# Attention and two MLP layers on one Trainium2 core: expert groups of four for the whole first layer, weight conversions spread out, and the last block's outputs finished one after the other

## The chip, the core and the metric

The kernel runs on one core of one Trainium2 chip (trn2). A core has five engines, each with a queue of its own that runs strictly in order: TensorE (PE, matrix products; PEld is its weight loading), VectorE (DVE), ScalarE (ACT), GpSimd (POOL) and SyncE (SP, which here issues all DMA transfers). They wait for one another through semaphores. Matrix products go to PSUM, from which ACT and DVE read them.

The metric is the device time of one execution in microseconds (us). Several runs are made; their median counts.

## What is computed

Three stages follow each other on 2304 tokens (4 batches of 576) of width 512:

```python
scores = q @ k.T / 8                         # 4 batches x 8 heads, 576 x 64
keep   = scores >= rowmax(scores) - tau
x      = softmax(where(keep, scores, -1e9)) @ v
x      = g(x @ w1_in) @ w1_out               # g(h) = h * sigmoid(1.702 h), 512 -> 2048 -> 512
out    = max(0.01 h, h) @ w2_out             # h = x @ w2_in
```

The arithmetic is float32. The weights arrive as 64-bit floats.

## The kernel before

**Products in parts.** The products are taken in the format fp32r, and every operand is split into a high part (a cast to it) and a low part (the difference); so every product is made three times: high by high, low by high, high by low. In the names, `xh`/`xl` are the two parts of a layer's input, `wih`/`wil` of its input weights, `gh`/`gl` of the hidden values, `woh`/`wol` of its output weights. The cast is ACT's (L318, L294, L827), the difference mostly POOL's (L320, L297, L828).

**Attention** handles 16 head pairs. Its instructions stand in an order written out by hand: the table `START` gives a number to each step of each pair, and the steps are emitted by ascending number (`G20` is the load of an input-weight tile, `H0` and `H1` are hidden sums of the first layer, which already run among the last pair's steps). Three weight tiles are converted in attention (`CONVERTED`), three more are only loaded there (`STAGED`).

**The MLP layers** work on blocks of 512 tokens (`TB`; five blocks, the last of 256) and on hidden slices of 128 (`f`, 16 per layer). The slices are taken in groups (`GROUPS`): for each group, all five blocks go by, and for each block all slices of the group. One (group, block, slice) is a step. In step s, PE makes the hidden sums of step s (`hidden_sums`, L332: 12 matmuls) and then the output products of step s - 2 (`product`, L856 or, in layer 2, L858: 12 matmuls), since `LA` is 2. Between the two, ACT applies the nonlinearity (L820 or L823), DVE completes it (L821 or L824), ACT casts it to `gh`, POOL makes `gl`. After a block's last slice in a group, `collect` adds the output sums to an accumulator that lies where the block's input lay (L874 copies for the first group, L876 adds, L879 and `store` for the last group of layer 2). Layer 1 has groups of 2, 4, 4, 4 and 2 slices, layer 2 four groups of 4. An undisturbed step of 512 tokens is 24 matmuls of 512 columns.

**Weight conversion.** Each (slice, in or out) weight tile of 128 by 512 is loaded as 64-bit words (G, L261, into one of three staging buffers `w64`), and turned into float32 by integer operations in five parts: A on ACT (L275), B, C, D, K on DVE (L277, L279, L283, L287), all in a tile `wF` (two buffers); then H, the high part, on ACT (L294) and M, the low part, on POOL (L297). Two plans say in which steps the parts are emitted:

```python
    slow = dict(G=-4, A=0, B=1, C=1, D=2, K=2, H=3, M=3)
    fast = dict(G=-2, A=0, B=0, C=0, D=0, K=0, H=0, M=0)
```

The slow plan takes a new tile every second step; the fast one does a whole tile in every step, and is used where a stretch has too few steps for the slow one: for the first group's missing tile (step 0), for group 1's eight tiles (steps 1 to 8, beside group 0's ten steps), and for layer 2's first eight tiles (beside layer 1's last group, ten steps). `weight_parts` emits them: A to K and H stand in a step after the nonlinearity and ahead of the cast `gh` of that step. So the ACT queue holds in a fast step: nonlinearity, A, H (which waits for DVE's K), `gh`, splits.

**Splits of the input.** `splits(s)` emits the split of the next block's input in the first group of each layer, four chunks over the present block's steps; block 1 of layer 1 is split ahead of step 0.

**The end.** Block 4 has 256 tokens and, in layer 2, two output tiles of 128 tokens. Both lie in one PSUM tile. The last two products run one after the other, each over both outputs, and then both are added and stored (two transfers each).

What is written after the hand-ordered part may be placed by the program's scheduler among earlier instructions where nothing holds it; within an engine's queue the order is then fixed.

## Time and profile before

| quantity | us |
|---|---|
| runs: lowest, median, highest (3) | 1187.96, 1189.27, 1189.45 |
| the profiled execution's own time | 1188.86 |
| its span, first to last instruction | 1187.1 |
| PE busy in the span | 1133.6 (95%) |
| DVE busy | 663.6 (56%) |
| ACT busy | 586.3 (49%) |
| POOL busy | 586.3 (49%) |
| mean granted TensorE clock | 0.986 of full speed |

The profiled execution lies 0.41 us under the median, and its span 1.76 us under its own time; those 1.76 us lie around the span. A busy PE is not a PE at full speed: matmuls overlap in the records, and at a lower granted clock (1.2 instead of 2.4 GHz) a busy PE does half the work. In the profile, "chain" is the chain of waits that ended last, followed back from the last instruction; a timeline row gives in brackets the idle time ahead of an instruction and who ended it.

### The profile page before, as it was taken

What the parts mean: (1) busy time and instruction counts of PE and PEld (TensorE: products, weight loads), DVE (VectorE), ACT (ScalarE), POOL (GpSimd) and SP (SyncE); (2) the same over time, 40 slices, a digit from 0 to 9 for tenths busy, and PEclk for the clock granted to TensorE, in tenths of its full rate; (3) what the DMA queues carried; (4) which work ended last, traced back from release to release, by engine and by line L of the source; (5) the groups of instructions that cost most, each with busy time, mean ns of one, the idle gap of its engine ahead of it and who ended that gap; (6) DMA issues with size and microseconds to landing.
All of it is one profiled execution on the core that took longest, in us unless ns stands there. A gap on an engine that the chain in (4) does not pass through costs nothing.

```text
span 1187.1 us, 17037 instructions
## 1 busy us (share of the span) xinstructions
PE 1133.6 (95%) x6201; PEld 968.2 (82%) x6201; DVE 663.6 (56%) x1357; ACT 586.3 (49%) x1138; POOL 586.3 (49%) x519
## 2 busy tenths in 40 slices
PE   8998999999896799999999999889999999999997
PEld 7887898889884588888888888778888888888886
DVE  6999999999876633443452524843343352534232
ACT  6998989999884432332332322334433332332221
POOL 6787887877774423343343332455543333343221
PEclk8999999999997989999999999999999999999999
DMA  5332323221302201110110100211110110110022
GB/s 145 82 84 64 82 61 98 70 72 35 103 1 72 70 19 36 54 54 18 54 54 18 54 18 19 90 35 37 53 54 18 54 54 18 54 36 1 36 63 62
DMA packets 47619, 62.38 MB, mean 53 GB/s; under 512 B 10544, under 2 KB 39216, under 8 KB 47536
## 3 DMA queue, kind: packets, MB, share of 16 engines
q1 hardware_dynamic: 47536, 61.29, 18.3%
q8 instruction: 49, 0.80, 0.3%
q14 instruction: 34, 0.28, 0.1%
HBM read 47.71 MB, written 4.72 MB: 44 GB/s over the span
## 4 chain that ended last, share of the span: by engine, by line
PE 69%; DVE 14%; ACT 10%; issue 3%; POOL 2%; DMA 1%; SPq 0%; DVEq 0%; ACTq 0%; POOLq 0%
PE h L332 30%; PE y L858 17%; PE y L856 13%; ACT e L469 3%; PE pv L585 3%; DVE m L462 3%; DVE pp L490 2%; PE s L435 2%; PE pp L511 2%; ACT raw L533 1%; DVE wF L277 1%; DVE wF L279 1%; DVE wF L287 1%; DVE x L876 1%; ACT ptg1h L542 1%
## 5 line engine op out<-in xcount | busy, mean ns | idle before, releaser
L828 POOL TENSOR_TENSOR gl<-gf,gh 128x512 fp32r<-128x512 f32 (+1 forms) x160 | 205.6, 1285 | 511.2 <-ACT gh L827 476.7
L824 DVE TENSOR_TENSOR gf<-h,gf 128x512 f32<-128x512 f32 (+1 forms) x80 | 51.0, 638 | 239.8 <-ACT gf L823 239.8
L332 PE MATMUL h<-xh,wih 128*128 128x512 f32 (+1 forms) x640 | 160.6, 371 | 17.5 <-ACT xh L318 17.5
L821 DVE TENSOR_TENSOR gf<-h,gf 128x512 f32<-128x512 f32 (+1 forms) x80 | 50.9, 637 | 207.6 <-ACT gf L820 207.6
L332 PE MATMUL h<-xl,wih 128*128 128x512 f32 (+1 forms) x640 | 160.8, 372 | 2.5 <-POOL xl L320 2.3
L823 ACT ACTIVATE gf<-h 128x512 f32<-128x512 f32 (+1 forms) x80 | 44.5, 556 | 233.8 <-PE h L332 230.7
L332 PE MATMUL h<-xh,wil 128*128 128x512 f32 (+1 forms) x640 | 159.2, 371 | 0.0
L332 PEld LDWEIGHTS h<-xh,wih 128*128 128x128 f32 x640 | 114.8, 188 | 41.7 <-ACT xh L318 20.5
L820 ACT ACTIVATE gf<-h 128x512 f32<-128x512 f32 (+1 forms) x80 | 44.4, 555 | 201.8 <-PE h L332 201.7
L332 PEld LDWEIGHTS h<-xl,wih 128*128 128x128 f32 x640 | 114.9, 191 | 25.0 <-POOL xl L320 5.0
L332 PEld LDWEIGHTS h<-xh,wil 128*128 128x128 f32 x640 | 114.7, 190 | 20.4
L856 PE MATMUL y<-gh,woh 128*128 128x512 f32 (+1 forms) x320 | 119.6, 378 | 8.1 <-DVE x L876 5.5
L827 ACT CAST gh<-gf 128x512 fp32r<-128x512 f32 (+1 forms) x160 | 92.5, 578 | 59.6 <-DVE gf L824 33.6
L856 PE MATMUL y<-gh,wol 128*128 128x512 f32 (+1 forms) x320 | 118.4, 374 | 0.0
L469 ACT ACTIVATE e<-s,m 128x576 f32<-128x576 f32 x144 | 110.8, 772 | 11.4 <-DVE m L462 10.2
L462 DVE TENSOR_REDUCE m<-s 128x1 f32<-128x576 f32 x144 | 107.7, 751 | 13.1 <-PE s L435 8.4
L858 PE MATMUL y<-woh,gh 128*128 128x512 f32 x288 | 112.4, 390 | 0.0
L858 PE MATMUL y<-wol,gh 128*128 128x512 f32 x288 | 112.3, 390 | 0.0
L435 PE MATMUL s<-kt,qt 128*128 128x288 f32 x512 | 100.3, 318 | 10.2 <-DVE pp L490 5.4
L490 DVE SCALAR_TENSOR_TENSOR pp<-s,thr,e 128x576 f32<-128x576 f32 x128 | 103.4, 810 | 7.9 <-ACT e L469 6.6
L856 PE MATMUL y<-gl,woh 128*128 128x512 f32 (+1 forms) x320 | 91.7, 371 | 0.0
L435 PEld LDWEIGHTS s<-kt,qt 128*128 128x128 f32 x512 | 73.2, 191 | 21.5 <-DVE pp L490 12.3
(117 smaller groups left out, 2209.0 us busy)
## 6 DMA issues: line engine op xcount, KB each, us to landing
w<-in_moe_w_in_dram SPq DMA_DIRECT2D x32, 512.0 KB, 3.6
w<-in_moe_w_out_dram SPq DMA_DIRECT2D x32, 512.0 KB, 3.6
kt<-kt SPq DMA_DIRECT2D x30, 288.0 KB, 4.1
kn<-in_k_dram SPq DMA_DIRECT2D x16, 256.0 KB, 2.9
qn<-in_q_dram SPq DMA_DIRECT2D x16, 256.0 KB, 2.9
vn<-in_v_dram SPq DMA_DIRECT2D x16, 256.0 KB, 3.0
out_dram<-o SPq DMA_DIRECT2D x20, 128.0 KB, 2.4
out_dram<-o SPq DMA_DIRECT2D x8, 256.0 KB, 2.2
```

The source lines that it names most:

```text
L332: nc.tensor.matmul(h, lhsT=wt[:, c * P : (c + 1) * P], rhs=xx[c], start=i == 0 and c == 0, stop=i == 2 and c == NCB - 1)
L435: nc.tensor.matmul(sc[:, a, 0:HALF], lhsT=w, rhs=kt[n][:, c : c + HALF], start=n == 0, stop=n == 1)
L462: nc.vector.tensor_reduce(out=small(p, "m")[:, t : t + 1], in_=r["s", t][:, :, 0:HALF], axis=mybir.AxisListType.XY, op=ALU.min)
L469: nc.scalar.activation(split(e, 2), r["s", t][:, :, 0:HALF], AF.Exp, bias=r["m"][:, t : t + 1], scale=-1.0)
L490: nc.vector.scalar_tensor_tensor(out=split(dst, 2), in0=r.pop(("s", t))[:, :, 0:HALF], scalar=r["thr"][:, t : t + 1], in1=split(r.pop(("e" ...
L821: nc.vector.tensor_tensor(out=gf, in0=h, in1=gf, op=ALU.mult)
L823: nc.scalar.activation(gf, h, AF.Copy, scale=0.01)
L824: nc.vector.tensor_tensor(out=gf, in0=h, in1=gf, op=ALU.max)
L827: nc.scalar.copy(gh, gf)
L828: nc.gpsimd.tensor_tensor(out=gl, in0=gf, in1=gh, op=ALU.subtract)
L856: nc.tensor.matmul(ys[e][:, 0:w], lhsT=wt[:, at_e], rhs=g, start=first, stop=last)
L858: nc.tensor.matmul(ys[e], lhsT=g[:, at_e], rhs=wt, start=first, stop=last)
```

## The change

- **Groups.** Layer 1 has four groups of four slices. The first group then needs eight weight tiles, of which three are converted in attention as before.
- **The five late tiles** of the first group are sorted by the step that needs them and planned one per step, with A two steps ahead, B to K one step ahead, H and M in the step. What falls ahead of step 0 is emitted before the loop (all of A to K of tile (2, in), and A of (1, out)). `wF` has three buffers. `STAGED` now loads (2, in), (3, in), (1, out) within attention.
- **All other tiles** follow the slow plan: a new one every second step.
- **Place in the step.** B to K stay where they were; H and M now come after the cast `gh` and POOL's `gl`, A at the end of the step, after the splits.
- **Splits.** Block 1 of layer 1 is split as the others are, a chunk per step in block 0's four steps.
- **Sigmoid's table.** Right after the last exponential of attention, a one-column sigmoid goes to ACT.
- **The end.** The last two products are made for output 0 first, which is added and stored, and then for output 1.

```diff
-GROUPS = {1: (2, 4, 4, 4, 2), 2: (4, 4, 4, 4)}
+GROUPS = {1: (4, 4, 4, 4), 2: (4, 4, 4, 4)}
-STAGED = ((1, 1), (2, 0), (2, 1))
+STAGED = ((2, 0), (3, 0), (1, 1))
...
-        "G21": 214030, "Lk": 281184, "Xh0": 294192, "dkh": 308029, "dkl": 309391, "Lq": 309466, "dqh": 311418,
+        "G11": 214030, "Lk": 281184, "Xh0": 294192, "dkh": 308029, "dkl": 309391, "Lq": 309466, "dqh": 311418,
...
-                floats[layer, f, n] = stg.tile([P, DM], F32, tag="wF", name=f"wF{layer}_{f}_{n}", bufs=2)
+                floats[layer, f, n] = stg.tile([P, DM], F32, tag="wF", name=f"wF{layer}_{f}_{n}", bufs=3)
...
             r["e", t] = e
+            if (p, t) == (NPAIR - 1, 8):
+
+                nc.scalar.activation(tau_b, tau_p, AF.Sigmoid)
...
-    def product(layer, blk, f, start, end):
+    def product(layer, blk, f, start, end, es=None):
...
-        order = [(e, i) for e in range(ne) for i in range(3)]
+        order = [(e, i) for e in es or range(ne) for i in range(3)]
...
-            todo.setdefault(max(0, s + d), []).append(item + (part,))
-
-    slow = dict(G=-4, A=0, B=1, C=1, D=2, K=2, H=3, M=3)
-    fast = dict(G=-2, A=0, B=0, C=0, D=0, K=0, H=0, M=0)
-    for i, item in enumerate(z for z in order[0] if z[1:] not in CONVERTED):
-        plan(item, i, fast)
+            todo.setdefault(max(-1, s + d), []).append(item + (part,))
+
+    late = [z for z in order[0] if z[1:] not in CONVERTED]
+    late.sort(key=lambda z: z[1] + (LA if z[2] else 0))
+    for i, item in enumerate(late):
+        plan(item, i, dict(G=-4, A=-2, B=-1, C=-1, D=-1, K=-1, H=0, M=0))
     for g, items in enumerate(order[1:]):
-        room = (first_step + [len(steps)])[g + 1] - first_step[g]
         for i, item in enumerate(items):
-            if room < 2 * len(items) + 3:
-                plan(item, first_step[g] + 1 + i, fast)
-            else:
-                plan(item, first_step[g] + 3 + 2 * i, slow)
+            plan(item, first_step[g] + len(late) * (g == 0) + 3 * (g > 0) + 2 * i, dict(G=-4, A=0, B=1, C=1, D=2, K=2, H=3, M=3))
...
-        if nxt >= len(steps) or steps[nxt][1] or (steps[nxt][0], steps[nxt][3]) == (1, 1):
+        if nxt >= len(steps) or steps[nxt][1]:
...
-    for c in range(NCB):
-        split_x(1, 1, c, nc.vector if c % 2 else nc.gpsimd)
+    weight_parts(-1, "GABCDK")
     for s in range(len(steps) + LA):
         weight_parts(s, "G")
         if s < len(steps):
             l, gi, size, blk, f, j = steps[s]
             rest = hidden(l, blk, f)
-            weight_parts(s, "ABCDKH")
+            weight_parts(s, "BCDK")
             rest()
-            weight_parts(s, "M")
+            weight_parts(s, "HM")
             splits(s)
-        if s >= LA:
+            weight_parts(s, "A")
+        if s >= len(steps):
+
+            if s == len(steps):
+                l, gi, size, blk, f, j = steps[-1]
+                ne = outputs(l, blk)
+                most, rest = range(ne - 1), (ne - 1,)
+                for g, es in ((f - 1, most), (f, most), (f - 1, rest), (f, rest)):
+                    product(l, blk, g, False, g == f, es)
+                    if g == f:
+                        collect(l, blk, gi, es)
+        elif s >= LA:
             l, gi, size, blk, f, j = steps[s - LA]
             product(l, blk, f, j == 0, j == size - 1)
             if j == size - 1:
                 collect(l, blk, gi)
```

Three places show how the instructions move. In the names, `wF1_2_0` is the converted tile of layer 1, slice 2, in (0) or out (1); `gf1_0_1` is layer 1, block 0, slice 1.

First ACT's queue within attention, where pair 14 ends and pair 15 begins (`e15_0` is the first exponential of pair 15); before, then now:

```order
L469 ACTIVATE e14_7_5081<-s14_7_5044,m14_4761 128x576 [waits DVE_49,Activation_49]
L533 COPY raw14_3_5088<-pp14_3_5022 128x512 [waits Pool_49]
L469 ACTIVATE e15_0_5092<-s15_0_5059,m15_5084 128x576 [waits DVE_49,Activation_49]
L413 ACTIVATE qt15_4863<-pt_q2_15_5015,qs_80 128x512
L600 COPY sh14_0_5103<-pv14_00_5069 64x256 [waits PE_49]
```

```order
L469 ACTIVATE e14_7_5081<-s14_7_5044,m14_4761 128x576 [waits DVE_49,Activation_49]
L536 COPY raw14_3_5088<-pp14_3_5022 128x512 [waits Pool_49]
L275 ACTIVATE wF1_2_0_5534<-w1_2_0_5174 128x512 [waits DMAHW0_49]
L275 ACTIVATE wF1_1_1_5540<-w1_1_1_3359 128x512
L469 ACTIVATE e15_0_5092<-s15_0_5059,m15_5084 128x576 [waits DVE_49,Activation_49]
L413 ACTIVATE qt15_4863<-pt_q2_15_5015,qs_80 128x512
```

The two A operations emitted ahead of the loop now stand here, the first behind its transfer; tile (2, in)'s B, C, D and K stand likewise on DVE, around the mask of `e15_0`.

Then ACT's queue at the start of the MLP, from attention's last copy (`sh15_1`) on; before, then now:

```order
L318 CAST xh1_1_3_5545<-x_77 128x512 [waits DMAHW7_49,DMAHW6_49]
L820 ACT_TABLE_LOAD
L820 ACTIVATE gf1_0_0_5549<-h1_0_0_5509 128x512 [waits PE_49]
L275 ACTIVATE wF1_1_1_5554<-w1_1_1_5174 128x512 [waits DMAHW0_49]
L294 CAST woh_1_1_5560<-wF1_1_1_5554 128x512 [waits DVE_49]
L827 CAST gh1_0_0_5550<-gf1_0_0_5549 128x512
L820 ACTIVATE gf1_0_1_5568<-h1_0_1_5428 128x512
L275 ACTIVATE wF1_2_0_5573<-w1_2_0_5411 128x512 [waits DMAHW4_49]
L294 CAST wih_1_2_5579<-wF1_2_0_5573 128x512 [waits DVE_49,Pool_49]
L827 CAST gh1_0_1_5569<-gf1_0_1_5568 128x512
```

```order
L603 COPY sh15_1_5489<-pv15_11_5483 64x320 [waits PE_49]
L823 ACTIVATE gf1_0_0_5546<-h1_0_0_5510 128x512 [waits PE_49]
L830 CAST gh1_0_0_5547<-gf1_0_0_5546 128x512 [waits DMAHW3_49,DMAHW4_49,DMAHW2_49,DMAHW5_49,DMAHW1_49,DVE_49]
L294 CAST wih_1_2_5557<-wF1_2_0_5534 128x512
L318 CAST xh1_1_0_5561<-x_77 128x512 [waits DMAHW7_49,DMAHW6_49]
L275 ACTIVATE wF1_3_0_5565<-w1_3_0_5411 128x512 [waits DMAHW4_49]
L823 ACTIVATE gf1_0_1_5569<-h1_0_1_5429 128x512
L830 CAST gh1_0_1_5570<-gf1_0_1_5569 128x512 [waits DVE_49]
L294 CAST woh_1_1_5580<-wF1_1_1_5540 128x512 [waits Pool_49]
L318 CAST xh1_1_1_5584<-x_77 128x512
L275 ACTIVATE wF1_2_1_5588<-w1_2_1_5542 128x512 [waits DMAHW5_49,Pool_49]
```

The four `xh` of block 1 and the table load are gone from the head (three of the four casts stand ahead of the first row before), `gh` stands right behind its nonlinearity, and H and A behind `gh`.

Last PE's queue at the end, where slice 14's products pass into slice 15's (`y2_12_4_0` is the PSUM tile of block 4 with both outputs; `gh2_4_14` and `gh2_4_15` are the last two slices); before, then now:

```order
L858 MATMUL y2_12_4_0_11652<-woh_2_14_10877,gl2_4_14_11647 128x512
L858 MATMUL y2_12_4_0_11652<-woh_2_15_11016,gh2_4_15_11673 128x512 [waits Activation_49]
L858 MATMUL y2_12_4_0_11652<-wol_2_15_11017,gh2_4_15_11673 128x512
L858 MATMUL y2_12_4_0_11652<-woh_2_15_11016,gl2_4_15_11674 128x512 [waits Pool_49]
L858 MATMUL y2_12_4_0_11652<-woh_2_15_11016,gh2_4_15_11673 128x512
```

```order
L861 MATMUL y2_12_4_0_11623<-woh_2_15_10989,gh2_4_15_11644 128x512 [waits Activation_49]
L861 MATMUL y2_12_4_0_11623<-wol_2_15_10990,gh2_4_15_11644 128x512
L861 MATMUL y2_12_4_0_11623<-woh_2_15_10989,gl2_4_15_11645 128x512 [waits Pool_49]
L861 MATMUL y2_12_4_0_11623<-woh_2_14_10852,gh2_4_14_11617 128x512 [waits DVE_49]
L861 MATMUL y2_12_4_0_11623<-wol_2_14_10853,gh2_4_14_11617 128x512
```

Output 1's first product of slice 14 now stands behind slice 15's for output 0, and waits for DVE, which then reads output 0 in the same PSUM tile.

## Rows read from the trace of the kernel before

**Rows 1.** Windows: length, busy us (count) by engine; granted clock; DMA share, GB/s.

```profile
352.04:431.10 79.06, 58.76 (x233) 45.72 (x230) 46.40 (x65) 34.20 (x65) 35.31 (x27) 0.85 0.20 60
431.10:728.65 297.55, 296.76 (x1441) 250.92 (x1441) 113.55 (x198) 89.70 (x162) 103.62 (x80) 1.00 0.12 36
728.65:794.26 65.61, 59.19 (x278) 47.22 (x277) 46.03 (x69) 24.36 (x45) 29.66 (x24) 1.00 0.21 65
794.26:1181.08 386.82, 386.21 (x1788) 322.17 (x1787) 139.67 (x235) 124.56 (x227) 146.56 (x117) 1.00 0.13 40
```

**Rows 2.** Waits of PE: start (2), layer boundary (1), layer 2 (1).

```profile
PE h L332 <- ACT xh L318: 15.8, 4, 6.3
PE y L856 <- ACT gh L827: 2.6, 1, 2.6
...
PE y L856 <- DVE x L876: 4.7, 6, 1.9
...
PE h L332 <- POOL xl L320: 0.6, 1, 0.6
```

**Rows 3.** Chain that ended last: start us, us, work. Two undisturbed pieces of PE.

```profile
429.67 1.43 PE y L856 x12
...
440.75 2.72 PE h L332 x12
```

**Rows 4.** The same chain at the start of the MLP: parts of its conversions.

```profile
366.65 0.69 DVE gf L821
...
367.81 1.41 DVE wF L279
369.25 0.70 DVE wF L283
...
378.03 0.62 ACT wih L294
```

**Rows 5.** Timeline, PE, after a wait: start us, us, line, operation, count.

```profile
380.86 1.91 PE L332 MATMUL h<-xh,wil 128*128 128x512 f32 x4
382.56 2.16 PE L332 MATMUL h<-xl,wih 128*128 128x512 f32 x4
```

**Rows 6.** Timeline, ACT, from the end of attention.

```profile
347.27 0.43 ACT L570 CAST rtg1h<-pr 128x320 fp32r<-128x320 f32 x1 [0.61 <-PE pr L556]
348.12 0.59 ACT L533 COPY raw<-pp 128x512 f32<-128x512 f32 x1 [0.43 <-PE pp L511]
...
354.31 1.28 ACT L820 ACT_TABLE_LOAD   x1
355.60 0.60 ACT L820 ACTIVATE gf<-h 128x512 f32<-128x512 f32 x1
```

**Rows 7.** Timeline, POOL, first step of the MLP.

```profile
360.44 1.29 POOL L828 TENSOR_TENSOR gl<-gf,gh 128x512 fp32r<-128x512 f32 x1 [4.64 <-ACT gh L827]
361.69 1.46 POOL L297 TENSOR_TENSOR wol<-wF,woh 128x512 fp32r<-128x512 f32 x1
```

**Rows 8.** Timeline, SP and ACT, pair 15's beginning; landing of SP's two weight loads.

```profile
317.51 0.72 SPq L261 DMA_DIRECT2D w<-in_moe_w_out_dram  x1
...
DMA to landing us min/median/max: 4.0/4.5/4.9
...
322.60 0.74 ACT L469 ACTIVATE e<-s,m 128x576 f32<-128x576 f32 x1 [0.94 <-DVE m L462]
```

**Rows 9.** Timeline, DVE: the same first operations of a conversion, quick and slow.

```profile
356.87 0.41 DVE L277 TENSOR_SCALAR wF<-wF 128x512 f32<-128x512 f32 x1
357.32 0.43 DVE L279 TENSOR_SCALAR wF<-wF 128x512 int32<-128x512 int32 x1
...
755.13 1.44 DVE L277 TENSOR_SCALAR wF<-wF 128x512 f32<-128x512 f32 x1
```

**Rows 10.** Timeline, all engines, the end.

```profile
1181.11 1.29 DVE L879 TENSOR_TENSOR o<-y,x 128x512 f32<-128x512 f32 x2 [3.20 <-PE y L858]
1181.83 2.40 SPq L894 DMA_DIRECT2D out_dram<-o  x4
```

More of the change, by code (lines that the diff above doesn't have):

```diff
@@ L844, in product @@
         ys = y_of[layer, blk]
-        gh, gl = g_of.pop((layer, blk, f))
+        gh, gl = g_of[layer, blk, f]
         woh, wol = wslot[layer, f, 1]
         kinds = ((woh, gh), (wol, gh), (woh, gl))
-        order = [(e, i) for e in range(ne) for i in range(3)]
+        order = [(e, i) for e in es or range(ne) for i in range(3)]
         if not end:
@@ L858, in product, with collect @@
                 nc.tensor.matmul(ys[e], lhsT=g[:, at_e], rhs=wt, start=first, stop=last)
-    def collect(layer, blk, gi):
+    def collect(layer, blk, gi, es=None):
         cols = span(blk)
         w = cols.stop - cols.start
-        for e, y in enumerate(y_of.pop((layer, blk))):
+        for e, y in enumerate(y_of[layer, blk]):
+            if e not in (es or range(NCB)):
+                continue
             if layer == 1:
```

4 rows, old and new, of the table START are left out of this document.

## The prediction

> **What bounds the kernel now.** Read the windows first [rows 1]. They cut the MLP into the start, the rest of layer 1, the boundary between the layers, and layer 2. Then take PE's undisturbed pieces from the chain [rows 3]: 12 matmuls of 512 columns take 2.72 us, of 256 columns 1.43. With the program's steps counted against them, each window shows what it lost:
>
> - Start, 79.06 us: 16 pieces of 2.72 and 3 of 1.43 are 47.8 us of work, so 31.3 are lost. PE was idle for 79.06 - 58.76 = 20.3 of them; the other 11.0 went to matmuls at the lower clock (granted 0.85 on average).
> - Rest of layer 1, 297.55 us: 96 of 2.72 and 24 of 1.43 are 295.4, lost about 2.1 over three group changes.
> - Boundary, 65.61 us: 18 of 2.72 and 5 of 1.43 are 56.1, lost 9.5.
> - Layer 2, 386.82 us: 125 of 2.72, 16 of 1.43 and 16 half pieces (block 4's two outputs) of 1.36 are 384.7, lost 2.1.
>
> So the MLP is PE bound nearly everywhere, and 40.8 of its 45.0 lost us lie in two windows: the two in which tiles are converted by the fast plan. PE's waits there [rows 2] are put down to the cast `xh` (15.8 us in four waits), to `gh` once (2.6), and at the boundary to DVE's collect (4.7). The chain [rows 4] says what held these: behind one slice's nonlinearity (0.69) DVE does a whole conversion (L279 alone 1.41, L283 and L287 0.70 each), then ACT casts it (0.62); `gh`, `xh` and the collect stand behind that in ACT's and DVE's queues. After such waits PE restarts at 1.2 GHz: four matmuls of 512 take 382.56 - 380.86 = 1.70 us [rows 5], against 0.91 at 2.4 GHz.
>
> **The change, part by part.**
>
> *Start.* Nine conversions in nine steps become five, none of which holds a `gh` any more; the eight of the next group go into every second step, as in the windows that lose next to nothing. What is left is slices 2 and 3 of block 0, whose weights come just in time. I follow PE from the first hidden sum in the window. Up to step 5 it has seven pieces, 19.0 us. After the first: nonlinearity 0.60 [rows 6], DVE 0.69, `gh` 0.62 and the cast of tile (2, in) 0.62 [rows 4] come in turn, so PE waits about 2.6. Its low part needs POOL's `gl` 1.29 and M 1.46 [rows 7] behind `gh`; that is 2.1 after PE's restart, of which four matmuls cover 0.9: wait 1.2. Eight matmuls at 1.2 GHz cost 1.6 more than at 2.4. Slice 3: from the end of slice 2's sums, 0.60 + 0.69 + 0.62 + 1.29 + 1.46 = 4.7, of which one product (2.72) and four matmuls cover 3.6: wait 1.0. The last chunk of block 1's split has one more POOL operation of 1.29 behind these, 5.95 against 5.2 of cover: wait 0.75. Together 7.15; with 0.35 for the clock's way back, 7.5. Saved: 31.3 - 7.5 = 23.8. Bounds: from below 4, where the chains overlap better and the clock stays up; from above the present price, 31.3/9 = 3.5 for each of five, 17.4. I take 7.5, since the queue order no longer puts `gh` behind a conversion.
>
> *Boundary.* Layer 2's first eight tiles get 20 steps instead of ten, and block 0's split four steps instead of two. The nearest rows are layer 2's own group changes, and its narrow block with a split beside it, where PE waited once, 0.6 us [rows 2]. I take 0.6; bounds 0 and 3. Saved: 9.5 - 0.6 = 8.9.
>
> *One collect fewer, H and A moved, a third `wF`.* Twenty additions on DVE leave; DVE was not what PE waited for outside the two windows, so this is nothing. H and M one cast later have five steps in hand before their group begins. In the steady steps, POOL's `gl` and M, 2.75 us, lie beside 5.4 us of PE: nothing either.
>
> *Attention pays.* Two A on ACT and four operations on DVE now stand in pair 15's beginning. SP issues the load at 317.51, and the slower of two landings took 4.9 us, so A can begin at 322.4 at the earliest; the exponential behind it began at 322.60 after 0.94 us of idling [rows 8]. DVE's four are 0.41 + 0.43 [rows 9] + 0.70 + 0.70 = 2.24 quick, and 4.25 when the first two are slow (1.44 in rows 9, 1.41 in rows 4). Taken: 2.24 less half of the idle time, 1.8. Bounds 0.5 and 4.25. The rows show the first operation between 0.41 and 1.44, the slow one while POOL works. The Trainium skill ("SBUF — State Buffer", "Who interferes with whom") has a rule that speaks against the move: such an operation and one of POOL's exclude each other for their whole length. By it, with POOL busy there, the sum would be 2 us worse, 1160.6; the trace agrees that both lengths occur.
>
> *Sigmoid's table.* The load takes 1.28 us, and the next activation begins right behind it [rows 6]. Moved, it no longer delays the first `gf` (left out of the start above). In attention it stands ahead of two idle gaps of 0.61 and 0.43 [rows 6]: bounds 0 and 1.28, taken 0.4. The Trainium skill ("ScalarE: Activation LUTs", "What ACT_TABLE_LOAD costs") adds a drain of 1.38 us to each load. By that the cost could be 1.4 higher, 1160.0; the row shows no such pause.
>
> *The end.* Output 0 is ready after 12 of the last 18 matmuls, its addition takes about 0.65 of the 1.29 for two [rows 10], but output 1's six matmuls now wait for that addition, since both outputs share a PSUM tile. PE ends some 0.95 later. SP's four stores, 0.6 each [rows 10], were in a row behind the first addition; now only two follow the last addition. Last issue: -0.2. Bounds -0.8 and +0.8.
>
> *Sum.* -23.8 - 8.9 + 1.8 + 0.4 - 0.2 = -30.7. Against the profiled execution's 1188.86 that is 1158.2; the median of the runs lies 0.41 higher, so **1158.6 us**.
>
> **Rivals.**
>
> 1. *Each late conversion keeps its present price.* They are still serial over ACT, DVE and POOL, and (2, out)'s load can only start when (1, out) is converted, with ACT's A waiting for it. Then the start loses 17.4, not 7.5: 1168.5. Against it: the long waits of now follow from the order in the queues, which is gone. Chance 0.15.
> 2. *The boundary is not the conversions'.* Its waits name the collect and the split, both still there, in a narrow block. If they keep all 9.5: 1167.5. Against it: layer 1's other group changes have the same collect and lose 0.7 each. Chance 0.05.
> 3. *The change doesn't do what it says at the start*: the four waits named `xh` are the splits' own, and spreading conversions frees nothing. Then 23.8 are missing: 1182.4. Against it: two casts take 1.05 of waits of 4 to 6 us, conversions the rest. Chance 0.04.
> 4. *Slower: the spread conversions hold PE in the steady steps.* H and A stand later, so M is later by a cast and a half, 1.1 us, in each of 56 tiles. If PE had no slack there, it would lose 61.6: 1220.2. It decides from 30.7/56 = 0.55 us per tile. Against it: the same plan without that shift runs in windows that lose 2.1 us each in all, and the weights are five steps early. Chance 0.02.
>
> **How the numbers follow.** The forecast has 0.74, and its own range is 1153 to 1164: the lower end with a start of 4 (-3.5) and attention at 0.5 plus 0 (-1.7), the upper with slow operations and the table load in full (+3.3) and the boundary at 3 (+2.4). The range takes in rivals 1 and 2: 1153 to 1169, which leaves out rivals 3 and 4 and some of the forecast's own tails, some 0.14 in all. 0.2%, about what a measurement of this kernel can tell from no change, is 2.4 us. All cases but the fourth rival are faster by more than that: faster 0.97, same 0.01 (gains and costs that happen to cancel), slower 0.02.
>
> **What would show it.** In the changed profile: step 5's hidden sum (block 1, slice 1) begins near 380.8 us; PE's waits between 354 and 377 sum to 5 to 6 us, first on ACT's `wih` cast, then on POOL's `wil`; no wait over 1 us at the boundary; the table load stands within attention with nothing idle behind it; the first hidden sum begins near 354.2 instead of 352.04; at the end PE waits about 0.8 us for DVE. I am wrong if the start's granted clock stays near 0.85 up to 400 us, if ACT waits for the load of (2, out) longer than slice 2's sums last, or if attention ends more than 5 us later.

## The result, and the profile after

| quantity | before | changed |
|---|---|---|
| median of the runs, us (4 each) | 1188.77 | 1168.85 |
| lowest and highest | 1187.96, 1189.45 | 1167.08, 1170.02 |
| ratio to before, 95% interval | | 0.9834 (0.9819 to 0.9850) |
| the profiled execution's time, its span | 1188.86, 1187.1 | 1167.08, 1165.3 |

The change is worth 1.7%, some 19.8 us, where 30.7 were forecast. The profiled execution is the fastest of the four. Its attention ran ahead from the start: the last `kt` copy that SP issues in attention (called SP's last copy below) stands at 315.23, against 315.82 to 318.15 in the twelve other profiles below and 316.81 before. Read prices from differences inside a profile, and add this head start of about 1.6 us.

The windows, as in [rows 1]: start, rest of layer 1, the boundary from layer 1's last narrow block to layer 2's first, the rest.

```profile
353.82:386.86 33.04, 24.68 (x88) 18.45 (x85) 22.30 (x23) 12.50 (x24) 18.91 (x13) 0.85 0.20 64
386.86:745.77 358.91, 357.52 (x1706) 300.45 (x1704) 144.82 (x253) 124.11 (x224) 146.56 (x114) 1.00 0.13 43
745.77:846.55 100.78, 100.03 (x482) 83.36 (x480) 38.12 (x67) 43.58 (x83) 60.06 (x48) 1.00 0.13 42
846.55:1160.48 313.93, 312.55 (x1465) 261.64 (x1463) 114.77 (x193) 92.84 (x168) 105.89 (x85) 1.00 0.14 41
```

The start is now 33.04 us for seven pieces of 2.72, 19.04 of work: **14.0 us lost, not 7.5**. Counted in the same way, the boundary window loses 2.3 (32 pieces of 2.72 and 8 of 1.43 make 98.48), and the other two windows lose 3.6 and 2.7, the end's 0.9 among them. Of the 14.0, PE was idle for 33.04 - 24.68 = 8.4; the other 5.6 went to matmuls at the lower clock.

PE's waits in the start window (us in total, times, longest), answering [rows 2]:

```profile
PE h L332 <- ACT wih L294: 5.0, 2, 2.6
PE h L332 <- POOL wil L297: 2.6, 2, 1.3
PE h L332 <- POOL xl L320: 0.8, 1, 0.8
```

PE in order of time, as [rows 5]:

```profile
359.41 1.19 PE L332 MATMUL h<-xh,wih 128*128 128x512 f32 x4 [2.58 <-ACT wih L294]
361.93 2.08 PE L332 MATMUL h<-xh,wil 128*128 128x512 f32 x4 [1.32 <-POOL wil L297]
...
370.57 1.20 PE L332 MATMUL h<-xh,wih 128*128 128x512 f32 x4 [2.40 <-ACT wih L294]
373.07 2.07 PE L332 MATMUL h<-xh,wil 128*128 128x512 f32 x4 [1.31 <-POOL wil L297]
...
383.74 0.50 PE L332 MATMUL h<-xl,wih 128*128 128x512 f32 x1 [0.75 <-POOL xl L320]
...
386.86 1.07 PE L332 MATMUL h<-xh,wih 128*128 128x512 f32 x4
```

Slice 2's two waits are those of the forecast (2.6 and 1.2). Slice 3's were forecast as 1.0 together and are 3.7; behind them PE runs at 1.2 GHz up to 378. Step 5 begins at 386.86, where 380.8 was named. DVE's and POOL's rows of that time show why:

```profile
359.02 1.74 DVE L283 SCALAR_TENSOR_TENSOR wF<-w,wF 128x512 int32<-128x512 int32 x1
360.79 1.64 DVE L287 SCALAR_TENSOR_TENSOR wF<-w,wF 128x512 int32<-128x512 int32 x1
362.35 0.68 DVE L824 TENSOR_TENSOR gf<-h,gf 128x512 f32<-128x512 f32 x1
362.95 0.91 DVE L277 TENSOR_SCALAR wF<-wF 128x512 f32<-128x512 f32 x1
363.90 1.44 DVE L279 TENSOR_SCALAR wF<-wF 128x512 int32<-128x512 int32 x1
365.37 1.66 DVE L283 SCALAR_TENSOR_TENSOR wF<-w,wF 128x512 int32<-128x512 int32 x1
367.07 1.67 DVE L287 SCALAR_TENSOR_TENSOR wF<-w,wF 128x512 int32<-128x512 int32 x1
368.66 0.68 DVE L824 TENSOR_TENSOR gf<-h,gf 128x512 f32<-128x512 f32 x1
```

```profile
358.93 1.29 POOL L831 TENSOR_TENSOR gl<-gf,gh 128x512 fp32r<-128x512 f32 x1 [5.81 <-ACT gh L830]
360.17 1.71 POOL L297 TENSOR_TENSOR wil<-wF,wih 128x512 fp32r<-128x512 f32 x1
361.84 1.74 POOL L320 TENSOR_TENSOR xl<-x,xh 128x512 fp32r<-128x512 f32 x1
```

D and K (L283, L287) take 1.64 to 1.74 us here, not the 0.70 of [rows 4]. POOL is busy beside them nearly all the time, and its M and `xl` take 1.5 to 1.75 instead of 1.29 (`gl`, which begins ahead of D, stays at 1.29). A conversion is 4.2 to 5.7 us of DVE's work instead of 2.24, and the next slice's `gf` stands behind it: ACT has done its part of slice 2's at 366.09, DVE begins at 368.66.

SP's last copy and the load behind it, then ACT, in attention and at the MLP's first step, answering [rows 6, 8]:

```profile
315.23 0.60 SPq L418 DMA_DIRECT2D kt<-kt  x1
315.92 0.72 SPq L261 DMA_DIRECT2D w<-in_moe_w_in_dram  x1
```

```profile
321.67 1.25 ACT L275 ACTIVATE wF<-w 128x512 f32<-128x512 f32 x2 [1.60 <-DMA w<-in_moe_w_in_dram]
...
346.12 1.28 ACT L475 ACT_TABLE_LOAD   x1
347.42 0.20 ACT L475 ACTIVATE tau_b<-tau_p 128x1 f32<-128x1 f32 x1
...
356.87 0.60 ACT L823 ACTIVATE gf<-h 128x512 f32<-128x512 f32 x1 [3.01 <-PE h L332]
```

The two hoisted A wait 1.60 us for a load, and attention's exponentials wait behind them. The load was issued at 315.92, 5.75 ahead. The end, answering [rows 10], went as forecast:

```profile
1158.23 0.69 DVE L884 TENSOR_TENSOR o<-y,x 128x512 f32<-128x512 f32 x1 [1.85 <-PE y L861]
1158.95 3.56 SPq L899 DMA_DIRECT2D out_dram<-o  x4
1158.97 0.50 PE L861 MATMUL y<-woh,gh 128*128 128x512 f32 x1 [0.78 <-DVE o L884]
```

### The profile page after: what moved, and what is told of

It is laid out like the page before. It is cut to its first block, busy times and chain, and to the rows that moved or that the text cites. A ratio compares the mean times of both kernels' runs of the same rounds, so it can differ in the third digit from the quotient of the medians.

```text
span 1165.3 us, 16926 instructions
## 1 busy us (share of the span) xinstructions
PE 1127.4 (97%) x6201; PEld 966.4 (83%) x6201; DVE 639.7 (55%) x1327; ACT 589.2 (51%) x1139; POOL 602.7 (52%) x529
## 4 chain that ended last, share of the span: by engine, by line
PE 73%; DVE 10%; ACT 8%; issue 4%; POOL 2%; DMA 1%; SPq 1%; ACTq 0%; POOLq 0%; DVEq 0%
PE h L332 32%; PE y L861 17%; PE y L859 15%; ACT e L469 3%; DVE m L462 3%; PE pv L588 3%; DVE pp L493 2%; PE s L435 2%; PE pp L514 2%; ACT raw L536 1%; ACT ptg1h L545 1%; POOL xl L320 1%; ACT sh L603 1%; ACT kt L405 1%; DVE xs L611 1%
## 5 line engine op out<-in xcount | busy, mean ns | idle before, releaser
L831 POOL TENSOR_TENSOR gl<-gf,gh 128x512 fp32r<-128x512 f32 (+1 forms) x160 | 210.5, 1316 | 473.1 <-ACT gh L830 452.4
L332 PE MATMUL h<-xh,wih 128*128 128x512 f32 (+1 forms) x640 | 158.0, 369 | 5.0 <-ACT wih L294 5.0
L859 PE MATMUL y<-gl,woh 128*128 128x512 f32 (+1 forms) x320 | 88.5, 368 | 0.0
```

Of the source, the lines that this page charges most:

```text
L332: nc.tensor.matmul(h, lhsT=wt[:, c * P : (c + 1) * P], rhs=xx[c], start=i == 0 and c == 0, stop=i == 2 and c == NCB - 1)
L831: nc.gpsimd.tensor_tensor(out=gl, in0=gf, in1=gh, op=ALU.subtract)
L859: nc.tensor.matmul(ys[e][:, 0:w], lhsT=wt[:, at_e], rhs=g, start=first, stop=last)
```

## The experiments

Each starts from the changed kernel. "Start" is the time from the first sums of the MLP, those that stand last in attention's table (353.82 above; "the first sums" below), to step 5's (386.86): 33.04 in the changed kernel, of which 19.04 is work. Times are compared by the difference of the ratios to before, 0.9834 for the changed kernel, times 1188.8 us.

Times also move for a reason outside the start: in the profiles of e4, e5, e6, e11 and e12 the granted clock (the seventh number) fell within attention, to 0.80 to 0.92 between 296 and 308, where the changed kernel and the others have 1.00 (in e3 to e6 it fell between 323 and 334 too). The changed kernel, then e5:

```profile
296.00:308.00 12.00, 10.07 (x78) 8.92 (x77) 10.16 (x26) 10.03 (x21) 8.49 (x8) 1.00 0.31 80
```

```profile
296.00:308.00 12.00, 10.23 (x68) 9.45 (x66) 9.06 (x22) 8.79 (x18) 8.73 (x10) 0.86 0.39 97
```

e4 to e6 leave attention as it is, and their first sums come some 2 us later than in the changed kernel, counted from the same copies ahead of 296. Why the clock fell there isn't shown. So the column "start" is the cleaner measure of what an edit did at the start.

| run | median us | ratio, 95% interval | start |
|---|---|---|---|
| e1 POOL freed | 1164.20 | 0.9793 (0.9779 to 0.9808) | 27.70 |
| e2 (3, in) before (1, out) | 1164.19 | 0.9793 (0.9778 to 0.9807) | 28.65 |
| e3 first sums exchanged | 1167.28 | 0.9820 (0.9806 to 0.9835) | 30.40 |
| e4 boundary put back | 1178.97 | 0.9921 (0.9904 to 0.9937) | 33.01 |
| e5 H and M first | 1166.99 | 0.9810 (0.9795 to 0.9824) | 30.05 |
| e6 waits filled | 1168.65 | 0.9826 (0.9812 to 0.9841) | 31.44 |
| e7 table in place | 1168.31 | 0.9826 (0.9811 to 0.9841) | 32.68 |
| e8 e2, e3, e5 together | 1162.00 | 0.9772 (0.9755 to 0.9788) | 26.57 |
| e9 loads early | 1167.08 | 0.9818 (0.9805 to 0.9831) | 32.80 |
| e10 e8 and e9 | 1161.49 | 0.9775 (0.9762 to 0.9789) | 26.56 |
| e11 one more in attention | 1164.40 | 0.9790 (0.9776 to 0.9803) | 27.20 |
| e12 e11, two PSUM tiles | 1162.92 | 0.9790 (0.9773 to 0.9806) | 25.87 |

**e1: are D and K slow because of POOL?**

```diff
-            nc.gpsimd.tensor_tensor(out=wl, in0=F, in1=wh, op=ALU.subtract)
+            if (layer, f, n) in late:
+                nc.scalar.copy(wl, F)
+            else:
+                nc.gpsimd.tensor_tensor(out=wl, in0=F, in1=wh, op=ALU.subtract)
...
-        if part != "h":
+        if part != "h" and (layer, blk) == (1, 1):
+            nc.scalar.copy(ls[c], x[c][:, cols])
+        elif part != "h":
...
```

> Starts from the changed kernel. The low parts of the five late tiles (M) and of block 1's split (xl) are written by ACT as plain copies, so they are not the differences that the reference needs; POOL keeps only gl in the first steps. In the changed kernel D and K (L283, L287) took 1.63 to 1.75 us each between 359 and 383 us, where 0.69 was measured before the change, and POOL was working beside them. Theory 1 (both engines slow each other): with POOL idle most of the time, those of D and K that lie outside gl take 0.7, conversion (3, in) on DVE shrinks from 5.8 us to about 3, the 2.40 us wait on its wih falls under 1, step 5 (block 1, slice 1) begins at 381 to 383 instead of 386.86, and the run is 4 to 6 us faster than the changed kernel's 1168.9. Theory 2 (DVE's row alone: the next gf stands behind a conversion, whatever POOL does): D and K stay near 1.7, only the waits on wil (1.3 each) and xl (0.75) go, and step 5 begins near 384.

Measured: 4.9 us faster, step 5 at 383.02. DVE and POOL, then PE and ACT at slice 3:

```profile
360.52 1.74 DVE L283 SCALAR_TENSOR_TENSOR wF<-w,wF 128x512 int32<-128x512 int32 x1
362.29 0.69 DVE L287 SCALAR_TENSOR_TENSOR wF<-w,wF 128x512 int32<-128x512 int32 x1
...
366.87 0.69 DVE L287 SCALAR_TENSOR_TENSOR wF<-w,wF 128x512 int32<-128x512 int32 x1
368.08 0.69 DVE L829 TENSOR_TENSOR gf<-h,gf 128x512 f32<-128x512 f32 x1 [0.52 <-ACT gf L828]
...
360.43 1.29 POOL L836 TENSOR_TENSOR gl<-gf,gh 128x512 fp32r<-128x512 f32 x1 [5.81 <-ACT gh L835]
...
370.00 2.07 PE L337 MATMUL h<-xh,wih 128*128 128x512 f32 x4 [3.35 <-ACT wih L294]
...
368.81 0.62 ACT L835 CAST gh<-gf 128x512 fp32r<-128x512 f32 x1 [0.76 <-DVE gf L829]
369.33 0.61 ACT L294 CAST wih<-wF 128x512 fp32r<-128x512 f32 x1
```

D, which still overlaps `gl`, takes 1.74; K, with POOL idle, 0.69, in all four conversions. That is theory 1: the neighbour sets the length. The 4.9 us are not the price of the lengths alone, since PE's waits for POOL's `wil` and `xl` went with them. And one of theory 1's numbers missed: the wait for slice 3's `wih` grew to 3.35. K of that tile ended at 367.56, and its cast H ran only at 369.33, because it stands behind `gh` in ACT's row, and `gh` waits for slice 2's `gf`. Some 0.5 of that is the experiment's own: ACT began that `gf` late, behind the copies added to its row, and DVE was idle for 0.52. So the place of H has a price too, and e5 was made for it.

**e2: the tile that is needed first**

```diff
-    late.sort(key=lambda z: z[1] + (LA if z[2] else 0))
+    late.sort(key=lambda z: z[1] + (LA + 0.5 if z[2] else 0))
```

> Starts from the changed kernel. One line: tile (3, in), needed by step 3's hidden sum, is converted before tile (1, out), needed by the product behind it. Theory 2 (the order in DVE's row sets the waits): conversion (3, in) takes the other's place and ends near 362.4, so the waits of 2.40 and 1.31 us at 370.57 and 373.07 go with the low clock behind them; what is left is about 2 us on wol of (1, out), whose M ends near 373; step 5 begins at 382 to 384 instead of 386.86, the run is 3 to 5 us faster than 1168.9. Theory 1 alone (two slow conversions of 5 to 6 us take as long in either order): the product waits instead for what the hidden sum waited for, and no more than one product's time, 2.7, is won: step 5 at 384 to 386.

Measured: 4.9 us faster, start 28.65 (4.4 less). Slice 3's waits are gone; 1.9 is left on `wol` of (1, out), as expected, and 1.0 on `xl`. The conversions stay as long as before. Two tiles had the same key in the sort, and the one for the later product came first.

**e3: slice 0's sums first in attention**

```diff
-        "T8": 393935, "l6": 394479, "E8": 397228, "H1": 397397, "S8": 398444, "a01": 398677, "w7": 398909,
+        "T8": 393935, "l6": 394479, "E8": 397228, "H0": 397397, "S8": 398444, "a01": 398677, "w7": 398909,
...
-        "rb1": 445769, "N1": 446614, "a11": 452586, "b11": 456244, "H0": 465212, "c1": 475832,
+        "rb1": 445769, "N1": 446614, "a11": 452586, "b11": 456244, "H1": 465212, "c1": 475832,
```

> Starts from the changed kernel. Attention's table has slice 1's hidden sums at 344.66 and slice 0's at 353.82; here the two names change places, so that slice 0's are there first. In the changed kernel ACT's first gf waits 3.0 us for the sums that end at 356.54. Theory 2 (a chain in the rows of ACT and DVE that begins with the first gf): gf of slice 0 now starts near 354, conversion (1, out) ends 2.5 to 3 us earlier, PE's first wait of 2.58 falls under 0.5, and everything behind moves with it: step 5 begins at 383 to 384.5, the run is 2.5 to 3.5 us faster than 1168.9. Rival: the first gf is held by the release of attention's buffers as well, and nothing moves by more than 0.5 us. Theory 1 says nothing on it beyond that the lengths of D and K stay 1.6 to 1.75.

Measured: start 2.6 less, the time 1.7 less, where 2.5 to 3.5 were expected, with an interval that overlaps the changed kernel's. The first `gf` started at once and the first wait of 2.58 vanished; but slice 3's wait on `wih` rose from 2.40 to 3.74, so half of it came back. The next wait in the row was right behind.

**e4: only the boundary put back**

```diff
-GROUPS = {1: (4, 4, 4, 4), 2: (4, 4, 4, 4)}
+GROUPS = {1: (4, 4, 4, 2, 2), 2: (4, 4, 4, 4)}
...
+            if (first_step + [len(steps)])[g + 1] - first_step[g] < 2 * len(items) + 3:
+                plan(item, first_step[g] + 1 + i, dict(G=-3, A=-1, B=0, C=0, D=0, K=0, H=0, M=0))
+            else:
...
```

> Starts from the changed kernel. Only the boundary between the layers is put back: layer 1 ends with two groups of two blocks, where the next group's tiles are converted one per step by the fast plan (A one step earlier, B, C, D, K, H and M in one step), with the changed order inside a step. In the kernel before, this boundary lost 9.5 us (rows 1); in the changed kernel the hundred us around it lost 2.3. If the price is that of one conversion per step, it loses about 9 again, and one more group change 1.0: 8 to 9 us slower than the changed kernel, 1177 to 1178. If the order inside a step was the cause, it loses at most 3: 1170 to 1172.

Measured: 10.3 us slower, more than the 8 to 9 expected. PE's waits from 400 us on, then the ten steps of each of the two groups of two slices:

```profile
PE y L859 <- ACT wF L275: 4.3, 4, 1.9
PE y L859 <- DVE x L881: 3.5, 4, 1.3
```

```profile
662.68:715.03 52.35, 50.14 (x242) 41.58 (x241) 29.07 (x44) 15.87 (x29) 17.73 (x15) 1.00 0.13 41
715.03:772.25 57.22, 52.45 (x241) 42.62 (x240) 41.84 (x63) 22.16 (x40) 24.04 (x20) 0.97 0.24 74
```

Each of the two is 49.24 us of work (16 pieces of 2.72, 4 of 1.43), so they lose 3.1 and 8.0. So one conversion per step costs nearly what it cost before, with the new order inside the step as well: ACT's A, DVE's conversion and the collect still stand between a slice and its `gh`. Which of them each product waited for isn't shown: the rows name A, which no product reads.

But the edit does more than put the boundary back. It also converts the last group's four tiles one per step, beside the group ahead, where the kernel before used the slow plan; that is part of the 3.1. And D takes 1.74 in eleven of these twelve conversions, where the kernel before had 0.69 at its boundary. So 10.3 is too much for the boundary's part alone; by the windows, 9.5 lost before and 2.3 now, it is worth some 7 us.

**e5: H and M ahead of `gh` and `gl`, as H was before**

```diff
-            rest()
-            weight_parts(s, "HM")
+            if s < len(late):
+                weight_parts(s, "HM")
+            rest()
+            if s >= len(late):
+                weight_parts(s, "HM")
```

> Starts from the changed kernel. For the five late tiles H (ACT) and M (POOL) stand ahead of the step's gh and gl again, as H did before the change. My prediction gave the later place a price of nothing. Theory 3 (that place has a price at the start): H of (2, in) follows the first gf at once, so the first wait falls from 2.58 to about 1.3 and the wait of 1.32 on its wil to under 0.3; H of (3, in) follows K and its M follows at once, so 2.40 becomes about 1.2 and 1.31 under 0.5; with the low clock behind these waits, step 5 begins 30 us or less behind slice 0's sums instead of 33.0 (386.86 - 353.82), and the run is 3 to 5 us faster than 1168.9. By theories 1 and 2 (DVE's slow conversions, and their order) what PE waits for is the end of a conversion on DVE: the waits for slice 3 stay within 0.5 us of 3.7 and no more than 2 us are won.

Measured: start 3.0 less, 2.9 us faster (the intervals just overlap).

```profile
PE h L332 <- ACT wih L294: 6.4, 2, 5.2
PE h L332 <- POOL wil L297: 0.5, 1, 0.5
```

Slice 2's waits became 1.19 and 0.51, where about 1.3 and under 0.3 were expected. Slice 3's wait on `wih` did not shrink: 5.20 instead of 2.40, since PE got there earlier, and the sums began only 0.8 us earlier behind the first ones (372.81 - 356.87 against 370.57 - 353.82). What came behind went: the waits on slice 3's `wil` and on `xl`, and part of the low clock. So theory 3 holds for slice 2 and for M; the end of (3, in)'s conversion is DVE's, as theories 1 and 2 say.

**e6: no idle PE, useless matmuls in its waits**

```diff
...
+            for c in range(keep[i] if i < len(keep) else 0):
+                nc.tensor.matmul(spare, lhsT=wslot[1, 0, 0][0][:, 0:P], rhs=hs[c % NCB], start=True, stop=True)
```

> Starts from the changed kernel. PE gets 31 matmuls of 512 columns with no use, written to a spare PSUM tile that nobody reads: 11 ahead of slice 2's sums, 5 ahead of their wil part, 10 and 5 at slice 3's, as many as fit its waits of 2.58, 1.32, 2.40 and 1.31 us at 0.227 us each. Theory 4 (a good part of the loss is the clock: 16 matmuls of sums took 3.36 and 3.58 us where 1.81 each is the quick price, and a product 3.69 instead of 2.72, 4.3 us in all): the granted clock stays at 1.0 up to 390 us, step 5 begins 28.5 to 30 us behind slice 0's sums instead of 33.0, and the run is 3 to 4.5 us faster than 1168.9. If the waits alone count, because what follows waits for ACT, DVE or POOL anyway, no more than 1 us is won.

Measured: start 1.6 less, the time 1.0 less with an interval that overlaps. The same window in the changed kernel and here, where the first sums begin at 357.03 (the seventh number is the granted clock):

```profile
354.00:390.00 36.00, 27.64 (x98) 20.90 (x99) 22.19 (x23) 13.07 (x24) 22.05 (x15) 0.86 0.19 59
```

```profile
354.00:390.00 36.00, 32.21 (x143) 24.92 (x143) 22.92 (x25) 13.93 (x27) 22.43 (x17) 1.00 0.18 59
```

The clock stayed at 2.4 GHz throughout, and of the 5.6 us that the changed kernel's start lost to it 1.6 came back: PE then waits 1.5 for `wih` and 1.6 for `xl`. Matmuls at 1.2 GHz lay mostly beside work that was late anyway. Whether the 11.0 us that [rows 1] show as lost to the clock would behave in the same way was not tried.

**e7: the table load left ahead of the first `gf`**

```diff
-            if (p, t) == (NPAIR - 1, 8):
-
-                nc.scalar.activation(tau_b, tau_p, AF.Sigmoid)
```

> Starts from the changed kernel without the one Sigmoid behind the last exponential, so that the table is loaded ahead of the first gf again. In the changed kernel that gf waits until 356.87 for sums that end at 356.54, while ACT is idle from 353.9: the load of 1.28 us lies in idle time there, and in attention it was put ahead of a cast. So either nothing (within 0.5 us), or up to 1.28 us faster with slice 0's sums beginning that much earlier. If my prediction's step is right that the load was on the start's path, it is about 0.5 to 1 us slower.

Measured: no difference that the runs can tell.

```profile
354.65 1.28 ACT L820 ACT_TABLE_LOAD   x1
357.64 0.60 ACT L820 ACTIVATE gf<-h 128x512 f32<-128x512 f32 x1 [1.71 <-PE h L332]
```

The load lies in time in which ACT waits for the sums anyway. The preload gains nothing here. Its cost in attention, from SP's last copy to the first sums, is 0.4 (38.20 here, 38.59 in the changed kernel), as forecast; but e1, with the changed kernel's attention, has 39.00, so 0.4 is also the spread between profiles.

**e8: e2, e3 and e5 together**

> Starts from the changed kernel; three changes of order together: (3, in) converted before (1, out), slice 0's sums exchanged with slice 1's in attention's table, H and M of the late tiles ahead of gh and gl. By theory 2 with 3 the waits of slice 2 go (each under 0.5 us), slice 3 finds its weights ready, and what is left is up to 3 us on (1, out) and 1 on the last xl; step 5 begins 23 to 26 us behind the last sums in attention (33.0 now), the run is 7 to 9 us faster than 1168.9: 1160 to 1162. By theory 1 alone (two slow conversions take as long in every order) the gain is no more than that of the second run, 4.7 us: 1164.

Measured: 7.4 us faster than the changed kernel, start 26.57 (23 to 26 was expected), so 7.5 lost.

```profile
PE y L859 <- ACT woh L294: 2.0, 1, 2.0
PE h L332 <- POOL xl L320: 1.3, 1, 1.3
PE y L859 <- POOL wol L297: 0.9, 1, 0.9
```

Waits on slices 2 and 3 are gone, and this is more than any of the three alone gives, but less than their sum: the start is 6.5 shorter, and 4.4, 2.6 and 3.0 were won one by one. The conversions are still 5.0 to 5.2 us each, and what is left hangs on the second of them, (1, out).

**e9: loads early, and places behind them**

```diff
-        "G11": 214030, "Lk": 281184, "Xh0": 294192, "dkh": 308029, "dkl": 309391, "Lq": 309466, "dqh": 311418,
+        "G20": 214030, "G11": 225000, "G30": 240000, "Lk": 281184, "Xh0": 294192,
+        "A20": 300000, "B20": 309400, "C20": 312600, "D20": 314600, "K20": 324000, "A11": 316000, "dkh": 308029, "dkl": 309391, "Lq": 309466, "dqh": 311418,
...
```

> Starts from the changed kernel; nothing of the MLP's start is changed. The loads of the three staged tiles are issued at the end of pair 10 instead of in pairs 10, 15 and 15, and the A and DVE parts that stand in attention get fixed places in pair 15's table, far behind their loads. In the profiles of the changed kernel and of all runs so far the hoisted A stood 1.6 to 2.2 us in ACT's row waiting for a load whose issue came 5.7 to 6.3 us earlier, and the first sums of the MLP began 37.5 to 38.9 us behind that issue (37.9 in the changed kernel) where the kernel before took 34.53 (352.04 - 317.51). Theory 5 (attention's price was mis-sized: 3 to 4 us, and half of it is this wait): no wait of ACT for a weight load, and 1.5 to 2.2 us faster than 1168.9. If the wait is hidden behind other work of attention: within 0.5 us of 1168.9.

Measured: 1.9 us faster, interval overlapping. ACT no longer waits for a load, and the first sums begin 36.31 us behind SP's last copy in attention: 38.59 in the changed kernel, 35.23 before (352.04 - 316.81). So attention's price was 3.4 in the changed kernel, and by this distance 2.3 of it go. But most of that is only paid ahead of the copy, where both A and DVE's B, C and D now stand:

```profile
307.26 0.78 DVE L284 SCALAR_TENSOR_TENSOR wF<-w,wF 128x512 int32<-128x512 int32 x1
317.53 1.38 DVE L288 SCALAR_TENSOR_TENSOR wF<-w,wF 128x512 int32<-128x512 int32 x1
```

Counted from the `kt` copy two before, which stands ahead of every moved part (263.77 in the changed kernel, 264.07 here, 265.32 before), the first sums come after 90.05, 89.29 and 86.72 us. So the price is 3.3, and early loads win 0.8 of it. This run does not separate the wait from the other places of the DVE parts.

**e10: e8 with e9's loads.**

> The eighth run's kernel with the loads and places of the ninth. If the prices add, 1.5 to 2.2 us faster than the 1162.0 there, near 1160; if the wait for the load is hidden, 1162.

Measured: 0.9775, not to be told from e8's 0.9772. The first sums begin 36.29 behind the last copy as in e9, but a gain of about 0.8 is too small to show in the runs.

**e11: (3, in) converted wholly in attention** (`A30` to `K30` and `A11` in the table, the late tiles' A to K one step earlier).

> The tenth run's kernel with the late tiles one step earlier: (3, in) is converted wholly in attention, A of (1, out) too, and DVE's row at the start has three conversions behind gf instead of four. In the eighth run the start lost 2.04 and 0.92 us to waits on (1, out), 1.30 on xl, and some 2.6 to the low clock behind them. If DVE's slow conversions (5.0 to 5.2 us each there) are what is left at the start, the waits on (1, out) go and with them the low clock: 4 to 6 us less at the start against 2.2 to 4.3 more in attention (the four operations at their quick and slow lengths), so between 0 and 3 us faster than the tenth. If attention's DVE has no room, the same or up to 1 us slower.

Measured: 1.8 us slower than e10 (the intervals overlap), where at most 1 was expected. The first sums come 39.06 behind the last copy instead of 36.29, so four more operations on DVE and one on ACT cost attention 2.8, and the start gains nothing: 27.20 against 26.56. Two waits are left there:

```profile
PE y L862 <- POOL wol L298: 2.1, 1, 2.1
PE h L333 <- ACT xh L319: 1.8, 1, 1.8
```

**e12: the last block's two outputs in PSUM tiles of their own** (on top of e11).

> The eleventh run's kernel, and in the last group the two outputs of block 4 lie in PSUM tiles of their own. In the changed kernel PE waits 0.78 us for DVE's addition of output 0 before output 1's last six matmuls. The wait goes, the addition of output 0 runs beside them: 0.8 to 0.9 us faster than the eleventh if DVE and SP do not become the end, which is what the last rows show (SP's last two stores follow the last addition either way).

Measured: the wait of 0.78 ahead of the last six matmuls is gone from the rows, and one of 0.35 for another of DVE's additions has come at 1149.68; the ratio is e11's, 0.9790, so the runs neither show nor exclude 0.8 us. The start is 1.3 shorter than e11's, though nothing was changed there: between two profiles a start can differ by as much.

Best of all is e8 (e10 the same within its interval): 0.9772, 2.3% under the kernel before and 7.4 us under the change.

## Why the prediction's direction was right and its size wrong

Forecast 1158.6, measured 1168.85: 10.2 us short, 4.9 above the forecast's own range (1153 to 1164), and just inside the one that takes in rivals 1 and 2 (1153 to 1169). Term by term:

| term | forecast | measured | how |
|---|---|---|---|
| start, lost of 31.3 | 7.5 | 14.0 | window above |
| boundary and later, lost | 4.8 | 7.7 | windows above, without the end |
| attention and table, cost | 2.2 | 3.4 | distance from SP's last copy to the first sums |
| the end | -0.2 | -0.3 | PE ends 0.9 later, 4.8 us instead of 6.0 follow |

The misses are 6.5, 2.9, 1.2 and -0.1, together 10.5; the 0.3 more than 10.2 lie within the spread of the runs.

**What bounds the kernel: right.** PE does, and the two fast-plan windows held the loss.

**The boundary: right in kind, somewhat too large.** Forecast -8.9; the windows give 9.5 - 2.3 = 7.2, and e4's 10.3 has four more conversions and slower ones in it. Group changes cost more than my windows suggested, about 1.0 each in layer 1 and 2.3 at the boundary.

**The start: the step that failed** is "I take 7.5, since the queue order no longer puts `gh` behind a conversion". It still does, one engine further up: `gf` is DVE's before it is ACT's, and slice 1's and 2's `gf` stood behind a conversion in DVE's row. The sum for slice 3 has no term for that conversion; where the prediction does size one, in attention, it is 2.24 with D and K at 0.70. Mean lengths of D and K in the start window were 1.72 and 1.65, and slice 2's `gf` stood 2.57 behind (368.66 - 366.09). Of the 6.5 missed, 2.8 are such waits (8.4 of idle PE for 5.55) and 3.7 the lower clock behind them (5.6 for 1.95, eight matmuls and the way back); e6 shows that less than half of the second can be won without the first. In the old order POOL's work fell beside B and C (L279 at 1.41 in [rows 4]) and D and K ran while POOL was idle. The change moved them beside `gl`, M and all four chunks of `xl`. e1 shows that POOL is the cause of the lengths. The Trainium skill ("SBUF — State Buffer", "Who interferes with whom") says that a DVE instruction with two SBUF inputs contends with a GpSimd instruction that reads SBUF, for a port pair that is an exclusive lock. The rows agree: D and K, with two SBUF inputs, go from 0.69 to 1.7, POOL's M and `xl` from 1.29 to 1.7, and `gf`, with one input in PSUM, stays at 0.68. I weighed that rule in attention, where it gave 2 us, and not for D and K of the four conversions at the start.

**H and M moved: wrong.** I gave it nothing, for steady steps where it is nothing. At the start e5 shows 3.0 us: H of a tile whose conversion is done stands behind a `gh` that isn't. In e8 the orders together bring the loss to 7.5, the number forecast for the change; that it is the same number is chance.

**Attention: too cheap.** The four DVE operations were counted, the wait in ACT's row was not: A stood for a load issued 5.75 us earlier, where I took a landing after 4.9 and half of an idle gap to hide it. e9, without this wait, shows 0.8; the rest of the miss isn't taken apart.

**Rivals.** Rival 1 gave 1168.5, 0.4 from the result, with the right kind of cause (a serial chain over ACT, DVE and POOL) but the wrong place: A of (2, out) at 370.94 did not wait for its load. Its number is near by luck: it puts the start's loss at 17.4, which was 14.0, and the misses at the boundary and in attention make up for that. Rivals 2 to 4 fell: the boundary's loss went, PE's idle time at the start fell from 20.3 us to 8.4, and PE waits nowhere for a steady conversion.

**Marks.** First sums near 354.2: 353.82, a hit by luck, since without the head start of 1.6 it would be 355.4. No wait over 1 us at the boundary: 0.6 at most. 0.8 at the end: 0.78. Waits of 5 to 6 us up to 377: 7.6. Step 5 at 380.8: 386.86.

## What to carry to other kernels

Price a moved instruction by a row in which it stands beside its new neighbours; an instruction's length in an idle stretch is a lower bound. Follow a chain through every engine's row, not only through the one whose wait the profile names: each freed wait here (e3, e5, e11) exposed the next one in the row, and the three orders together gave less than their sum. At equal keys, sort by who needs a thing first.

## What was not expected of the hardware

An integer operation on DVE over two SBUF tiles of 128x512 took 0.69 us alone and 1.63 to 1.75 while POOL subtracted two SBUF tiles; POOL's took 1.29 alone and up to 1.75 then. With 31 useless matmuls in PE's waits the granted clock was 1.00 instead of 0.86 over 36 us, and the start was only 1.6 us shorter. The 512 KB load of tile (2, in), which I took to land after 4.0 to 4.9 us, landed and released its reader 5.7 to 6.3 us after its issue, in the changed kernel and in e1 to e8.
